# Two plain float32 pieces in block 0's first layer, all of W1 centred by means, loads on two queues, and a new written order

## The chip, the cores and the metric

One core of a Trainium2 chip. The time is device microseconds of one execution, the median of several runs. The kernel keeps all its engines under one written order: TensorE (PE) multiplies, VectorE (DVE), ScalarE (ACT) and GpSimd (POOL) do the elementwise work, SyncE (SP) issues the loads and stores.

## What is computed

A linear attention with decay over 4 batches, 8 heads and 768 tokens, in chunks, and on its output a normalised two-layer network with a residual:

```python
# attention, per chunk: y = ((C B^T) * L) x + (C state) * decay ;  state = decay * state + (B * decay)^T x
mu = np.mean(x, axis=-1, keepdims=True)
var = np.mean((x - mu) ** 2, axis=-1, keepdims=True)
xn = (x - mu) / np.sqrt(var + 1e-06) * g_ln
ch = np.maximum(xn @ w_ch1, 0.0) @ w_ch2          # 256 -> 1024 -> 256
return (x + ch).astype(np.float32)
```

## The kernel before

Tokens are cut into six blocks `t` of 128 tokens x 4 batches, so every matrix of a block has 512 columns. Per block the attention runs as scores `G`, weighting `R`, entering state `Vi`, values `V`, chunk sums `Z` and states `S`; `y` copies its result out of PSUM, `T` turns it by token, and the network follows: the first layer in eight pieces `h t m` of 128 rows, the second in four outputs `o t b` (for block 0 gathered in steps `oc 0 c j` that use one quarter of W2 at a time).

Precision is kept by splitting: a float32 value is an upper part in a short format (`wh` for weights, `yh` for values, `hh` for hidden values) and the rest (`wl`, `yl`, `hl`). A piece `h` multiplies upper by upper, lower by upper and upper by lower, over two halves k of 256 rows: six products of 512 columns (`hidden`, line 507).

The weights arrive as 64-bit words whose float32 content has to be decoded. For each of four tiles of W1 (`1 c k`: column half c, row half k) and four of W2 the steps are: `k0` (ACT) the magnitude, `k1` a clamp, `k2` a shift and `k3` the sign, all three on DVE, `kr` (ACT) the rest of the low word, and `f`, the sum of both, on DVE or POOL. The normalisation is folded into W1: W1 is centred over its rows. Half c=1 is centred on PE by products with `gd`, a diagonal less a mean (`wc`, line 237); half c=0 by a product that gives the mean (`wm`, line 242) and an addition on DVE (`wf`, line 247). Then `wh` and `wl` split it.

Other steps that are named here: `du` decays from the middle of a chunk, `cx`, `cm`, `C` scale C by them, `B` and `be` scale B, `W` writes decays into the weighting mask, `c2` scales C for the entering state, `sb` sets the state on the diagonal, `K` keeps the decayed state, `st` and `ag` are the row statistics, `oe` scales and adds the residual, `od` stores, `ru`, `riv`, `rd`, `ro`, `rcl` prepare the decays of later blocks, `fill` is an idle product on PE, `pc i` a tiny load on SP that waits for another load to land.

What sets the order: a string ISSUE, line 584, is read piece by piece; each engine gets its pieces in that order and works them off in that order. A letter behind a colon names the engine (`v` DVE, `p` POOL, `a` ACT, `s` SP); without one each step has a default. Tiles take a buffer from a pool that holds a set number; PE's first layer, the means and the outputs share three PSUM buffers (`ps_ffn`), freed when `hl`, `wf` or `oe` has read them.

Of the kernel before, what the change touches and what calls it, by code (L numbers as in the profile page):

```python
# [659 lines left out]
```

## Time and profile before

| | us |
|---|---|
| runs | 194.98, 195.91, 197.56 (median 195.91) |
| profiled execution, its own time | 194.59 |
| its span, first to last instruction | 192.6 |
| busy: PE, DVE, ACT, POOL | 185.3, 134.3, 67.4, 27.8 |
| share of the span: PE, DVE, ACT, POOL | 96%, 70%, 35%, 14% |
| granted TensorE clock | 1.00 throughout |

The span leaves out some 2 us of each execution ahead of the first and behind the last instruction. Busy time of PE counts pipelined products whose ends are modelled, so it says that PE had work and not that it was at its peak. A busy share over the whole span is an average over stretches that differ.

### The profile page before, as it was taken

Reading aid. Unit: us, or ns where it says so; the run is one execution under the profiler, and the core shown is the slowest. Engines: PE = TensorE matmul, PEld = TensorE weight load, DVE = VectorE, ACT = ScalarE, POOL = GpSimd, SP = SyncE. Lnnn points to the kernel's source line nnn. Section 1 sums busy time; section 2 is a strip of 40 time slices with the busy share of each in tenths; the row PEclk is TensorE's granted clock in tenths of the full one; section 3 lists DMA queues with packets and bytes.
Section 4 is the critical chain, followed back from the end, with each engine's and each line's share of the span. In section 5 each row is a group of like instructions: output and inputs, shape, how many; then the busy total and the mean of one; then the engine's idle time right before and its main releaser. Section 6 shows DMA issues by size and latency. Waiting matters only on the chain.

```text
span 192.6 us, 6374 instructions
## 1 busy us (share of the span) xinstructions
PE 185.3 (96%) x2834; PEld 159.2 (83%) x2834; DVE 134.3 (70%) x282; ACT 67.4 (35%) x132; POOL 27.8 (14%) x32
## 2 busy tenths in 40 slices
PE   8989799999999899999999999999999999999993
...
DVE  1699999999889687868899955636433772359321
...
DMA packets 11665, 18.42 MB, mean 96 GB/s; under 512 B 2390, under 2 KB 5878, under 8 KB 11638
## 3 DMA queue, kind: packets, MB, share of 16 engines
...
q8 instruction: 22, 0.36, 0.8%
...
## 4 chain that ended last, share of the span: by engine, by line
PE 82%; DMA 7%; DVE 4%; SPq 3%; issue 2%; POOL 1%; POOLq 0%
PE ph L513 32%; PE po L531 29%; PE yps L421 4%; DMA xt<-in_x_dram 4%; DMA b<-in_bn_dram 3%; PE yt L482 3%; PE G L394 3%; PE yps L413 3%; PE Z L433 2%; PE pp L541 2%; PE wc L240 2%; SPq L164 1%; SPq L149 1%; PE wm L245 1%; POOL top L225 1%
## 5 line engine op out<-in xcount | busy, mean ns | idle before, releaser
L531 PE MATMUL po<-w,hh 128*128 128x256 f32 x320 | 57.2, 281 | 0.0
L513 PE MATMUL ph<-yh,w 128*128 128x512 f32 x192 | 53.6, 401 | 0.5 <-DVE hl L524 0.5
L531 PEld LDWEIGHTS po<-w,hh 128*128 128x128 f32 x320 | 49.1, 188 | 0.7
L531 PE MATMUL po<-w,hl 128*128 128x256 f32 x160 | 44.7, 279 | 0.0
L513 PEld LDWEIGHTS ph<-yh,w 128*128 128x128 f32 x192 | 34.6, 188 | 8.3 <-DVE hl L524 0.9
L524 DVE SCALAR_TENSOR_TENSOR hl<-ph,hh 128x512 fp32r<-128x512 f32 x48 | 32.5, 680 | 9.9 <-ACT hh L518 9.6
L518 ACT ACTIVATE hh<-ph 128x512 fp32r<-128x512 f32 x33 | 19.4, 597 | 49.4 <-PE ph L513 42.5
L531 PEld LDWEIGHTS po<-w,hl 128*128 128x128 f32 x160 | 30.1, 188 | 0.0
L513 PE MATMUL ph<-yl,w 128*128 128x512 f32 x96 | 29.8, 391 | 0.0
L546 DVE SCALAR_TENSOR_TENSOR o<-po,rstd,ytok 128x256 f32<-128x256 f32 x20 | 9.5, 480 | 21.7 <-PE po L531 21.6
L513 PEld LDWEIGHTS ph<-yl,w 128*128 128x128 f32 x96 | 18.0, 188 | 4.0
L474 POOL TENSOR_TENSOR yl<-y,yh 128x512 fp32r<-128x512 f32 x6 | 8.1, 1351 | 59.7 <-DVE yh L471 37.9
L400 DVE TENSOR_TENSOR R<-G,WW 128x512 f32<-128x512 f32 x24 | 15.7, 678 | 1.1 <-PE G L394 1.1
L520 DVE TENSOR_SCALAR hh<-ph 128x512 fp32r<-128x512 f32 x15 | 10.3, 684 | 3.9 <-PE ph L513 3.8
L541 PE MATMUL pp<-w,hh 128*128 128x256 f32 x64 | 11.5, 281 | 0.0
L541 PEld LDWEIGHTS pp<-w,hh 128*128 128x128 f32 x64 | 9.9, 188 | 0.8 <-DVE cs L345 0.6
L457 ACT ACTIVATE sbd<-S,cst 128x128 f32<-128x128 f32 x10 | 3.5, 393 | 19.0 <-DVE S L449 19.0
L494 DVE BATCH_NORM_STATS2 st<-ytok 128x6 f32<-128x256 f32 x24 | 9.6, 413 | 0.0
L541 PE MATMUL pp<-w,hl 128*128 128x256 f32 x32 | 8.9, 279 | 0.5 <-issue 0.5
L558 PE MATMUL idle<-const-float32-0.0 128*128 128x256 f32 (+2 forms) x18 | 8.6, 601 | 0.8 <-PEq L648 0.8
L421 PE MATMUL yps<-R,xt 64*32 64x64 f32 x768 | 8.9, 225 | 0.0
L421 PEld LDWEIGHTS yps<-R,xt 64*32 64x32 f32 x768 | 7.9, 105 | 0.7 <-issue 0.4
...
## 6 DMA issues: line engine op xcount, KB each, us to landing
...
```

Of the source, the lines that this page charges most:

```text
L400: nc.vector.tensor_tensor(out=R.rearrange("p b i k -> p b (i k)"), in0=tiles.pop(("G", t, q)).rearrange("p b i k -> p b (i k)"), in1=WW.re ...
L421: nc.tensor.matmul(tiles["y", t, g, f][32 * k:32 * k + 32, b], x[r, b * NH + h], tiles["R", t, h // 2][r, b, h % 2], start=(t + f + b == 0 ...
L474: e.tensor_tensor(out=tiles["yl", t][:, g], in0=tiles["y32", t][:, g], in1=tiles["yh", t][:, g].bitcast(F32), op=ALU.subtract)
L494: nc.vector.bn_stats(out=st, in_=tiles["ytok", t][:, b])
L513: nc.tensor.matmul(ph, W1[m // 4, k][:, s, mc], v[:, k], start=(i == 0), stop=(i == len(cmb) - 1))
L518: e.activation(h, tiles["ph", t, m], AF.Relu)
L520: e.tensor_scalar(out=h, in0=tiles["ph", t, m], scalar1=0.0, scalar2=None, op0=ALU.max)
L524: nc.vector.scalar_tensor_tensor(out=l, in0=tiles.pop(("ph", t, m)), scalar=0.0, in1=tiles["hh", t, m].bitcast(F32), op0=ALU.max, op1=ALU. ...
L531: nc.tensor.matmul(po, tiles[v, t, m][:, cols], W2[m // 2,][:, s, (m % 2) * DM:(m % 2 + 1) * DM], start=(n == 0), stop=(n == len(cmb) - 1))
L541: nc.tensor.matmul(tiles["po", t, b], tiles[v, t, m][:, cols], W2[m // 2,][:, s, (m % 2) * DM:(m % 2 + 1) * DM], start=(c + n + b % 2 == 0 ...
L546: nc.vector.scalar_tensor_tensor(out=o, in0=tiles.pop(("po", t, b)), scalar=tiles["rstd", t][:, b], in1=tiles["ytok", t][:, b], op0=ALU.mu ...
L558: nc.tensor.matmul(ps[:, :n], zero.to_broadcast([P, P]), zero.to_broadcast([P, n]), start=True, stop=True)
```

## The change

Six edits. (1) Two of the eight pieces of block 0's first layer, m = 5 and 7, become `hf` (`hidden_plain`): two float32 products of the unsplit centred W1 and unsplit values. (2) Half c=1 of W1 is centred like half c=0: `wm 1`, `wf 1 0`, `wf 1 1` take the place of `wc 1 1`, `wc 1 0` and `gd`; `wh` and `wl` read it from SBUF. (3) The loads of `sel`, `sums`, `id` and `x 0` are issued by ACT. (4) The load of ACT's table moves from the start to just ahead of the logarithm. (5) Output tiles have four buffers for six, `y32` two for one; `lr` can run on DVE. (6) The whole order is written anew: which engine does what, the fills, and the `pc` loads. Cut to its core, with the orders up to the scores of block 2:

```diff
...
-    nc.scalar.preload_act_table_set("natural_log_exp_and_others")
...
-    op = pool("op", 6)
+    op = pool("op", 4)
...
-    gd = hp.tile([P, KC, P], F32, tag="hh", name="gd")
...
-    seen = cp.tile([1, 64], F32, name="seen")
+    seen = cp.tile([1, 176], F32, name="seen")
...
-    def clamped(w, *at):
+    def clamped(w, *at, e=nc.vector):
-        nc.vector.tensor_scalar(out=f, in0=f, scalar1=MIN_TOP, scalar2=MAX_TOP, op0=ALU.max, op1=ALU.min)
+        e.tensor_scalar(out=f, in0=f, scalar1=MIN_TOP, scalar2=MAX_TOP, op0=ALU.max, op1=ALU.min)
...
-    def centring(e=nc.vector):
-        if e is nc.scalar:
-            e.activation(gneg, gt, AF.Copy, scale=-1.0 / DM)
-            for k in range(KC):
-                e.activation(gd[:, k], ident, AF.Identity, bias=gneg[:, k:k + 1], scale=gt[:, k:k + 1])
-        else:
-            e.tensor_scalar(out=gneg, in0=gt, scalar1=-1.0 / DM, scalar2=None, op0=ALU.mult)
-            for k in range(KC):
-                e.tensor_scalar(out=gd[:, k], in0=ident, scalar1=gt[:, k:k + 1], scalar2=gneg[:, k:k + 1], op0=ALU.mult, op1=ALU.add)
-
-    def centred(c, k):
-        w = centre[c, k] = ps_ffn.tile([P, 512], F32, tag="ffn", name=f"wc{c}{k}")
-        for n, j in enumerate((k, 1 - k)):
-            nc.tensor.matmul(w, gd[:, k] if j == k else gneg[:, j:j + 1].to_broadcast([P, P]), f32[1, c, j], start=(n == 0), stop=(n == 1))
+    def centring(e=nc.scalar):
+        e.activation(gneg, gt, AF.Copy, scale=-1.0 / DM)
...
-        (e.copy if e is nc.scalar else e.tensor_copy)(t[:, 0], centre.get(at, f32[(w, *at)]) if w == 1 else f32[(w, *at)])
+        (e.copy if e is nc.scalar else e.tensor_copy)(t[:, 0], f32[(w, *at)])
-        e.tensor_tensor(out=t[:, 1], in0=centre.get(at, f32[(w, *at)]) if w == 1 else f32.pop((w, *at)), in1=t[:, 0].bitcast(F32), op=ALU.subtract)
+        e.tensor_tensor(out=t[:, 1], in0=f32[(w, *at)], in1=t[:, 0].bitcast(F32), op=ALU.subtract)
...
+        nc.scalar.preload_act_table_set("natural_log_exp_and_others")
...
-    def logs_repeated(t):
+    def logs_repeated(t, e=nc.scalar):
-        nc.scalar.activation(lr.rearrange("p (r n) -> p r n", n=DS), la[:, t].unsqueeze(2).to_broadcast([P, NR, DS]), AF.Copy)
+        (e.copy if e is nc.scalar else e.tensor_copy)(lr.rearrange("p (r n) -> p r n", n=DS), la[:, t].unsqueeze(2).to_broadcast([P, NR, DS]))
...
-            tiles["y32", t] = p1.tile([P, KC, TB], F32, tag="y32", name=f"y32{t}")
+            tiles["y32", t] = p2.tile([P, KC, TB], F32, tag="y32", name=f"y32{t}")
...
+
+    def hidden_plain(t, m):
+        ph = tiles["ph", t, m] = ps_ffn.tile([P, TB], F32, tag="ffn", name=f"ph{t}{m}")
+        for k in range(KC):
+            nc.tensor.matmul(ph, f32[1, m // 4, k][:, m % 4 * P:(m % 4 + 1) * P], tiles["y32", t][:, k], start=(k == 0), stop=(k == KC - 1))
...
-        k0=magnitude, k1=clamped, km=bounded, k2=shifted, k3=signed, kr=rest, f=whole, wc=centred, wm=mean_of, wf=less_mean, wh=upper, wl=lower,
+        k0=magnitude, k1=clamped, km=bounded, k2=shifted, k3=signed, kr=rest, f=whole, wm=mean_of, wf=less_mean, wh=upper, wl=lower,
-        h=hidden, hh=hidden_h, hl=hidden_l, o=outputs, oc=outputs_of, oe=finished, od=stored)
+        h=hidden, hf=hidden_plain, hh=hidden_h, hl=hidden_l, o=outputs, oc=outputs_of, oe=finished, od=stored)
...
...
-az, fill 0 512, ld la, inv, ld sums, ld mask, ld as, fill 1 512, ld b 0, l1, ini, ld id, l2, ld c 0, lr 0, ld bt 0, ones, fill 2 256, ld sel, rcl,
-ld g, ru, fill 3 64, ld w1 1 0, dc 0, ld w1 1 1, ld x 0, fill 4 256, du 0 1, e 1, du 0 0, B:v 0, fill 5 256, lr 1, so, cx 0 0, x 1, fill 6 256,
-cx 0 1, e 0, x 0, W:v 0, gm:a, G 0, pc 4 w1 1 0, k0 1 1 0, be:v 0, dc 1, ld w1 0 1, sm, k1 1 1 0, ld w1 0 0, mb, R 0 3, fill 7 512, du 1 0, ld bt 1,
-C 0, R 0 0, ld x 1, kr 1 1 0, sp, R 0 2, em 0, em 1, c2:p 0, Z 0 0, k0 1 1 1, riv, R 0 1, Z 0 1, S 0 0, k1 1 1 1, fill 8 256, sb:a 0 1, k2 1 1 0,
-k2 1 1 1, kr 1 1 1, Vi 0, k3 1 1 1, du 1 1, V 0 0, k3 1 1 0, k0 1 0 1, V 0 1, f:v 1 1 1, y 0 0 0, f:v 1 1 0, wc 1 1, y 0 1 0, kr 1 0 0, k1 1 0 1,
-ld c 2, ro 0, ld c 1, ld b 1, pc 2 w1 0 0, ld w2 0, k2 1 0 1, k0 1 0 0, k3 1 0 1, wc 1 0, be:v 1, k1 1 0 0, ld bt 2, k2 1 0 0, ld w2 2, rd, k3 1 0 0,
-ro 1, ld w2 1, f:v 1 0 0, ld x 2, K 0 1, ld b 2, C:v 1, ld ud 2, wh 1 1 1, kr 1 0 1, y 0 0 1, f 1 0 1, y 0 1 1, wh 1 1 0, T 0 1, yh:a 0 0, Z 1,
-yh:a 0 1, T 0 0, tc 0 1, yl 0 0, wm 0, W 1, wl:v 1 1 0, yl 0 1, S 0 1, wl:v 1 1 1, h 0 5, tc 0 0, K:p 1 0, wf 0 1, cm 1 1, B:v 1, h 0 4, cm 1 0,
-S 1 0, wf 0 0, k0 2 0, sb:v 1 1, G 1, hh 0 4, wh:v 1 0 1, wh 1 0 0, wl:v 1 0 1, hh 0 5, h 0 7, hl 0 4, wl 1 0 0, kr 2 0, hl 0 5, k0 2 2, R 1 0,
-h 0 3, sb 1 0, hh 0 7, R 1 2, c2:p 1, R 1 1, h 0 2, hh 0 3, K:p 1 1, hl 0 7, kr 2 1, B 2, st 0 1, S 1 1, h 0 1, R 1 3, C:v 2, k1 2 0, Vi 1, hh 0 1,
-st 0 2, cm:v 2 0, W 2, hl 0 1, V 1 0, c2 2, V 1 1, hl 0 3, h 0 0, y 1 0 1, ld x 4, k2 2 0, hh 0 2, ld w2 3, k3 2 0, y 1 0 0, ld c 3, y 1 1 1, cm 2 1,
-h 0 6, f:v 2 0, ld bt 3, yh:a 1 0, k1 2 2, K 2 0, y 1 1 0, yl:v 1 0, hh 0 0, G 2, yh:a 1 1, hl 0 2, hh 0 6, st 0 0, T 1 0, yl 1 1, R 2 3, wh 2 0,
...
+ld:a sel, fill 0 512, ld la, ld:a sums, ld mask, ld:a id, ld c 0, ld w1 1 0, fill 1 128, ld b 0, l1, fill 2 512, ini, ld bt 0, l2, ld:a x 0, lr:v 0,
+inv, ones:v, e 1, dc 0, x 1, W:v 0, so, du 0 0, fill 3 512, du 0 1, cx 0 1, sm, lr 1, mb, k0 1 1 0, cx 0 0, dc 1, ld w1 1 1, k1 1 1 0, e 0, B:v 0,
+x 0, du 1 0, C:v 0, G 0, kr 1 1 0, k2 1 1 0, be:v 0, sp, k3 1 1 0, em 0, Z 0 0, ld g, ld w1 0 0, ld as, ld c 1, ld w1 0 1, ld bt 1, ld b 1, c2:p 0,
+R 0 1, fill 4 256, S 0 0, R 0 3, sb:a 0 1, Z 0 1, f 1 1 0, R 0 0, k0 1 1 1, Vi 0, R 0 2, kr 1 1 1, V 0 0, az, k1 1 1 1, gm, du 1 1, k2 1 1 1, em 1,
+rcl, k3 1 1 1, k0 1 0 0, V 0 1, f:v 1 1 1, wm 1, y 0 1 1, pc 3 c 1, ld x 1, pc 19 c 0, pc 18 b 0, C:v 1, ld x 2, y 0 1 0, y 0 0 0, y 0 0 1, k1 1 0 0,
+cm 1 0, c2:p 1, wf 1 0, T 0 0, k0 1 0 1, T 0 1, wf 1 1, K:p 0 1, yh:a 0 0, hf 0 5, k2 1 0 0, kr 1 0 0, k1 1 0 1, ru, tc 0 1, k3 1 0 0, ro 0,
+wh 1 1 1, hf 0 7, ld w2 1, S 0 1, kr 1 0 1, k2 1 0 1, ld b 2, sb:a 1 0, be:v 1, ld w2 0, tc 0 0, k3 1 0 1, Z 1, cm 1 1, riv, f:v 1 0 1, yh:a 0 1,
+wl:v 1 1 1, hh 0 7, rd, W 1, ro 1, pc 15 b 2, wh:p 1 1 0, B 1, f 1 0 0, K:p 1 0, wm 0, yl 0 0, S 1 0, wl 1 1 0, hl 0 7, G 1, wf 0 0, ld c 2, yl 0 1,
+wf 0 1, ld bt 2, kr 2 1, h 0 4, ld ud 2, R 1 1, hh 0 5, wh:p 1 0 0, R 1 2, ld w2 2, K:p 1 1, R 1 3, h 0 6, hh 0 4, sb 1 1, S 1 1, k0 2 1, R 1 0,
+k0 2 0, Vi 1, k1 2 1, W 2, hl 0 4, hl 0 5, V 1 1, k1 2 0, V 1 0, K 2 0, k2 2 0, ld x 3, y 1 0 0, k3 2 0, y 1 1 1, ld c 3, y 1 1 0, y:v 1 0 1, hh 0 6,
+C:v 2, ld bt 3, hl 0 6, cm:v 2 0, yh 1 0, B:v 2, pc 11 w2 1, ld w2 3, ld ud 3, pc 13 w2 3, ld ud 4, ld b 3, wh:p 1 0 1, wl 1 0 0, wl 1 0 1, h 0 1,
+sb 2 0, be 2, h 0 0, hh 0 1, c2:p 2, cm 2 1, h 0 3, hh 0 0, yh:a 1 1, yl 1 0, hl 0 0, G 2, hh 0 3, k2 2 1, kr 2 0, yl 1 1, T 1 0, R 2 3, h 1 4,
+tc 1 0, hl 0 3, k3 2 1, h 1 2, f:v 2 0, hh 1 4, f 2 1, R 2 0, hl 1 4, Z 2, R 2 2, wh 2 1, T 1 1, hh 1 2, hl 0 1, h 0 2, st 0 0, wh:v 2 0, S 2 0,
+wl 2 0, h 1 3, sb:a 2 1, hh:v 0 2, kr 2 3, hl 0 2, tc 1 1, oc 0 0 1, K 2 1, kr 2 2, st 0 3, S 2 1, k0 2 2, ag 0 0, C:v 3, h 1 6, R 2 1, wl:v 2 1,
...
```

## Rows read from the trace of the kernel before

**Rows 1.** The page's 40 equal slices of the span, busy tenths.

```profile
PE   8989799999999899999999999999999999999993
DVE  1699999999889687868899955636433772359321
```

**Rows 2.** Busy us of each engine (instructions) in two stretches, clock, DMA share, GB/s.

```profile
20.00:25.00 5.00, 3.64 (x77) 2.15 (x76) 4.93 (x10) 3.52 (x9) 2.43 (x2) 1.00 0.87 295
30.00:35.00 5.00, 5.00 (x34) 4.05 (x22) 5.00 (x10) 3.69 (x7) 4.49 (x5) 1.00 0.22 75
```

**Rows 3.** The chain that ended last, in order: start us, us, what.

```profile
17.50 3.20 PE wc L240 x7
20.70 1.36 issue
24.57 1.72 PE wm L245 x4
...
43.05 2.78 PE ph L513 x12
...
189.25 0.48 DVE o L546
```

**Rows 4.** PE's instructions in order: start us, us, what, count, idle before.

```profile
25.72 1.50 PE L513 MATMUL ph<-yh,w 128*128 128x512 f32 x4
30.12 1.20 PE L513 MATMUL ph<-yh,w 128*128 128x512 f32 x4
41.26 1.21 PE L394 MATMUL G<-cm,bs 32*64 32x128 f32 x64
57.30 0.28 PE L541 MATMUL pp<-w,hl 128*128 128x256 f32 x1 [0.47 <-issue]
66.43 1.20 PE L513 MATMUL ph<-yh,w 128*128 128x512 f32 x4 [0.53 <-DVE hl L524]
```

**Rows 5.** The opening, in order of time: table load, fills, a load's issue.

```profile
0.73 1.28 ACT L82 ACT_TABLE_LOAD   x1 [0.73 <-PEq L648]
0.77 4.92 PE L558 MATMUL idle<-const-float32-0.0 128*128 128x512 f32 x8 [0.77 <-PEq L648]
1.18 0.42 SPq L164 DMA_DIRECT2D cf<-in_sums_dram  x1
1.76 0.34 PEld L558 LDWEIGHTS idle<-const-float32-0.0 128*128 128x128 f32 x1 [0.52 <-issue]
```

**Rows 6.** DVE and POOL side by side, in order of time.

```profile
20.86 1.40 POOL L225 TENSOR_TENSOR top<-top,low 128x512 int32<-128x512 int32 x1 [6.42 <-ACT low L220]
21.12 1.69 DVE L214 SCALAR_TENSOR_TENSOR top<-raw,top 128x512 int32<-128x512 int32 x1
...
31.56 1.88 DVE L400 TENSOR_TENSOR R<-G,WW 128x512 f32<-128x512 f32 x3
31.77 0.63 POOL L459 TENSOR_TENSOR sbd<-S,cst 128x256 f32<-128x256 f32 x1
...
44.80 0.64 POOL L459 TENSOR_TENSOR sbd<-S,cst 128x256 f32<-128x256 f32 x1
45.20 0.79 DVE L258 TENSOR_TENSOR w<-top,w 128x512 fp32r<-128x512 f32 x1
...
113.79 1.06 POOL L441 TENSOR_TENSOR K<-S,emt 128x256 f32<-128x256 f32 x1 [16.54 <-DVE S L449]
```

**Rows 7.** Groups by line and shape: count, busy us, mean ns of one, idle before.

```profile
L214 DVE SCALAR_TENSOR_TENSOR top<-raw,top 128x512 int32<-128x512 int32 x8 | 6.4, 805 | 0.1
L225 POOL TENSOR_TENSOR top<-top,low 128x512 int32<-128x512 int32 x3 | 4.0, 1326 | 7.4 <-ACT low L220 6.4 <-DVE top L214 1.0
L258 DVE TENSOR_TENSOR w<-top,w 128x512 fp32r<-128x512 f32 x5 | 3.6, 711 | 0.2
L368 POOL TENSOR_TENSOR c<-cs,em 128x512 f32<-128x512 f32 x4 | 4.2, 1049 | 22.4 <-DVE cs L345 22.4
L209 DVE TENSOR_SCALAR top<-top 128x512 int32<-128x512 int32 x8 | 3.3, 418 | 0.1
L441 POOL TENSOR_TENSOR K<-S,emt 128x256 f32<-128x256 f32 x5 | 3.5, 702 | 23.8 <-DVE S L449 23.8
```

More of the change, by code (lines that the diff above doesn't have):

```diff
@@ L617 @@
-oe 4 2, hh:v 5 1, hl 5 1, h 5 3, oe 4 1, od 4 1, h 5 0, hh 5 3, hl 5 3, h 5 4, hh 5 0, hl 5 0, h 5 6, hh:v 5 4, hl 5 4, h 5 7, ag 5 1, hh:v 5 6,
-hl 5 6, h 5 5, st 5 2, st 5 0, st 5 3, hh:v 5 7, hh 5 5, ag 5 2, hl 5 7, hl 5 5, o 5 2, ag 5 0, ag 5 3, rs 5, rc 5, o 5 1, o 5 3, oe 5 1, od 5 1,
-od 4 2, od 3 0, o 5 0, oe 5 3, oe 5 2, od 5 3, od 3 2, od 0 3, od 5 2, oe 5 0, od 5 0
+ld:a sel, fill 0 512, ld la, ld:a sums, ld mask, ld:a id, ld c 0, ld w1 1 0, fill 1 128, ld b 0, l1, fill 2 512, ini, ld bt 0, l2, ld:a x 0, lr:v 0,
```

41 lines of the change are left out of this document (21 added, 20 removed).

## Prediction, made before the changed kernel ran

> **What bounds the kernel now.** I read the page's 40 slices first, then the busy time by stretch, then the chain that ended last, and last the single instructions of VectorE and GpSimd. TensorE (PE) is busy in every slice but the first ones and the last [rows 1]. The stretches say what kind of busy it is: from 20 to 25 us PE is busy 3.64 us of 5 while VectorE (DVE) is busy 4.93; from 30 to 35 PE is at 5.00 of 5 and so is DVE [rows 2]. So the front, until the first layer of block 0 can start at 25.72 us, is paced by DVE; from there PE is full, and DVE runs close behind it until about 60 us and is half idle later [rows 1, 2, 4]. After 25.72 PE loses 1.0 us in two short waits, 0.47 ahead of 57.30 and 0.53 ahead of 66.43 [rows 4]. The last product ends at 189.2 us, one scaled addition of DVE and the stores follow, and the span ends at 192.6 [rows 3]. A gain must therefore come from an earlier, or a less broken, first part; PE idle time anywhere ahead of 189 us is lost for good, since PE works in written order.
>
> **What each matrix edit costs PE.** A first-layer piece with both values split is six products: twelve in 2.78 us, so 1.39 a piece. The mean of W1's half c is two float32 products that run as four instructions, 1.72 us [rows 3]. A plain piece `hf` is the same shape, so 1.72: two of them add 2 x 0.33 = +0.66 us. Replacing `wc 1 1` and `wc 1 0` (eight instructions, seven took 3.20, so 3.7 with the last [rows 3]) by one `wm 1` removes about 1.9 us. The fills shrink from 2880 to 1920 columns; they stood in the front, where PE waits anyway. Sum on PE about -1.2 us, all of it in the front, where PE doesn't set the pace: worth nothing by itself. The gain of `hf` is another: it needs no `wh`, `wl`, `yh`, `yl`, only float32 values and the centred half, so it can start earlier.
>
> **The front, along DVE.** ACT now issues three loads ahead of the table load. An issue takes 0.42 on SP, nearest row for ACT [rows 5]; from 0.73 three take until 2.1, the table 1.28 [rows 5] until 3.4, the logarithm after it (0.36) ends near 3.8. `lr:v 0`, `inv` and `ones:v` (0.6, 0.1, about 0.8 by its 1024 elements) fill DVE while it would wait for `x 1`, which hides them. `W:v 0` starts near 5.5. From there to the end of `wf 1 1` DVE has W 1.13, cx 2 x 0.65, B, C 0, be, k3, k3, f, C 1 at 0.60 each, four R at 0.60, six small ones at 0.34 (k1, k2 and `rcl`, 0.42 each [rows 7]), wf 2 x 0.66: 12.4 us with 0.7 of waits for ACT's `du` and `k0`, so about 18.7 us (start to start of operations in a row is 0.07 under the duration: three R in 1.88 [rows 6]). [...] The two plain pieces can run from 18.7 to 22, against a first piece at 25.72 before. This is the promise of the change, 6 to 7 us early; the question is whether the next piece follows.
>
> **What holds it back: GpSimd.** The new order moves work from DVE to GpSimd (POOL): counted over the two orders, `wl` 5 for 1, `wh` and `yh` 5 for none, `yl` 9 for 6, `sb` 4 for 2, one more each of be, K and W, one `c2` less: 43 operations for 27. POOL takes 1.33 us for a sum of 128x512, DVE 0.71 for the like [rows 7]; 16 more at some 1.1 are 18 us of POOL for about 9 of DVE and ACT. And the two don't run side by side. `k3` on DVE at 21.12 took 1.69 us, the other seven (6.4 - 1.69)/7 = 0.67: POOL's `f` lasted until 22.26 and `k3` ended 0.55 after it. `wl:v` at 45.20 took 0.79 while POOL's `sb` lasted until 45.44. In the other direction POOL's `K` of 113.79 took 1.06, behind a `yl:v` of DVE, where the mean of five is 0.70. The three R under POOL's work at 31.56 lost nothing: they read PSUM [rows 6, 7]. So a DVE operation with two SBUF inputs, or a fast single-input one, and a POOL operation exclude each other for their full length; DVE operations that read PSUM (R, S, hl, wf) are free. The order of before puts POOL's work under those. [...]
>
> [...] DVE: k2, k1, ru, k2 (4 x 0.34), k3, be 1, k3, f:v (4 x 0.60), 3.8 us. POOL, all needed soon: `wh:p 1 1 0` about 1.0 (not in the trace; between half of a two-input 1.30 and the whole; I take nearer the whole, since `c2` with one broadcast input takes 1.05 [rows 7]), B 1, f, yl and wl, each with two inputs, at 1.3 and K at 0.6 [rows 6, 7] (`sb`, as wide as K, 0.63), 6.8 us. Waiting engines take turns: POOL's `f` dispatched at 20.86 got in ahead of `k3` at 21.12 [rows 6]. So `f:v 1 0 1` ends at 18.7 + 10.6 = 29.4 (rounded up 0.1), not at 22.8. Behind it the second half of `wm 0` (0.86), G 1 (1.14): 31.4. Z 1 and `wm 0` stand in PE's order ahead of everything else, so PE idles between 22 and 31 for some 5 us. The third piece, `h 0 4`, also needs one of three PSUM buffers, freed by `hl 0 7`, which DVE reaches after yl (1.3 POOL), wl, rd, S, hl (1.9): 32.6. Before, the third piece started at 30.12 [rows 4]: +2.5 us.
>
> Next, `wl 1 0 1` gates piece (0,1): from 33.2 (`wf 0 0`) POOL does wh:p, K, sb, wh:p, wl, wl (5.8) and one k1 (0.34) gets between: 39.4. Then DVE, behind `hl 0 4` and `hl 0 5` (39.3), shares with sb 2 0 and be 2: 0.6 + 0.34 + 1.05 + K, k2, k3, y, C 2, hl, cm, yh, B 2 (4.6): B 2 ends near 45.9, and G 2 starts there. Before, G 2 started at 41.26 [rows 4] with eight pieces done; now with seven, so the same place would be 41.26 - 1.39 = 39.9. That is 6.0 us late. Behind it PE has more waiting for it than DVE, as now; the two waits of 1.0 us may vanish: +5.0.
>
> **The rest of the edits.** Four output buffers for six: the new order never holds more than four tiles, and a whole product `o` stands between a store and the next use of its buffer; nothing, and without that cover about the length of one addition, 0.48 [rows 3], a few times. The second `y32` buffer and the six tiny SP loads `pc` for three: SP waits there instead of elsewhere; what is queued behind are loads of block 2 and 3, needed after 40 us. x 0 on ACT's queue is needed at 11 us, by then under way for 7. Tail unchanged, 3.4 us. All at zero.
>
> **Sum.** Span 192.6 + 5.0 = 197.6. The profiled execution of before took 194.59, so 199.6 for one like it; the median shown is 195.91, 1.3 above, so I predict 200.9 us.
>
> **Rivals.** (1) The other side: POOL's operations fall under DVE's PSUM reads and cost DVE nothing. It decides if `f:v 1 0 1` ends before 25 us. Then `wm 0` ends at 23.7, G 1 at 24.9, the third piece starts at 25.5 instead of 30.12; `wl 1 0 1` at 32.5 and G 2 at about 36.2 against 39.9: 3.7 us early, and with the two vanished waits -4.7: 191.2. For it: the order of before shows that such packing works [rows 6]; against it: behind `wf 1 1` the new order has ten DVE operations in a row of which one reads PSUM. [...] (3) On top of the forecast PE falls to the slow pace: it was slow for its first 4.9 us [rows 5] and didn't fall after a wait of 1.36 us at 20.7 [rows 3]; the idle times I expect are longer. [...] Each fall costs at most the 2.5 us that 4.9 us at half pace lose: one to two falls, 203 to 206.
>
> **Chances.** Forecast (198.5 to 203) 0.42; rival 1 0.22; rival 2 0.22; rival 3 0.14. 2%, about what a measurement of this kernel can tell from no change, is 3.9 us: below 192.0 or above 199.8. Of rival 1, 0.17 lies below and 0.05 inside; rival 2 lies inside, and so does 0.10 of the forecast, its low end: faster 0.17, same 0.37, slower 0.46. Range: from rival 1's own figure, 191.2, to a little above rival 3's, 207.0; that leaves about 0.11 below and 0.03 above.
>
> **What would show it.** Right: `hf` near 19 to 20 us; then PE idle of several us before Z 1 and G 1; durations over 1 us among DVE's k1, k2, k3, be of 20 to 30 us and among POOL's; `h 0 4` after 31; G 2 after 44. Wrong, if POOL's busy time rises by 15 us and DVE's durations stay at 0.4 and 0.7, if G 2 starts before 40, or if a wait for a load or a store stands in the chain.

## The result: 1.2% slower, half of the forecast loss

| | before | after |
|---|---|---|
| median of 20 runs each, us | 195.91 (194.46 to 198.12) | 198.40 (196.70 to 201.06) |
| ratio, 95% interval | | 1.012 [1.0086, 1.0155] |
| profiled execution: time, span, us | 194.59, 192.6 | 200.21, 198.4 |
| busy: PE, DVE, ACT, POOL, us | 185.3, 134.3, 67.4, 27.8 | 188.9, 135.0, 64.5, 45.8 |

The change costs 2.5 us by the medians; 5.0 were forecast. The ratios leave out executions more than 1.5% above the quickest of their kernel, the medians are over all. The profiled execution of after is one of the longer of its twenty, so a second profile of the same kernel (`a0`, time 198.06, span 196.3) is used beside it; its four runs had a median of 198.98 and a ratio to before of 1.0225 [1.0155, 1.0295].

After, the page's 40 slices (they answer to [rows 1]):

```profile
PE   8997959997999999999999999999999999999993
DVE  3795599999999974877599684557441784238420
POOL 0043377767421290250000150200000500000000
PEclk9995795899999999999999999999999999999999
```

PE shows holes in the fourth and the sixth slice (15 to 20 and 25 to 30 us), the granted clock falls twice between 15 and 40 us (0.50 from 16 to 22, 0.53 from 29 to 36), and POOL is busy in the slices in which DVE is full. The stretches (busy us of PE, PEld, DVE, ACT, POOL, granted clock, DMA share, GB/s; [rows 2] has two of them before):

```profile
15.00:20.00 5.00, 3.63 (x116) 2.46 (x116) 2.74 (x6) 2.59 (x9) 1.73 (x2) 0.57 0.52 170
20.00:25.00 5.00, 5.00 (x16) 2.80 (x15) 2.96 (x4) 3.38 (x7) 2.07 (x2) 0.74 0.17 62
30.00:35.00 5.00, 4.66 (x26) 1.57 (x34) 4.96 (x7) 2.40 (x4) 3.32 (x2) 0.50 0.27 103
```

PE's instructions in order, after ([rows 4] before):

```profile
14.65 0.34 PE L408 MATMUL yps<-R,xt 64*32 64x64 f32 x14
16.37 1.86 PE L408 MATMUL yps<-R,xt 64*32 64x64 f32 x114 [1.39 <-issue]
18.16 3.78 PE L231 MATMUL wm<-top,gneg 128*128 128x512 f32 x4
23.03 3.60 PE L505 MATMUL ph<-y,top 128*128 128x512 f32 x8
...
28.89 1.01 PE L420 MATMUL Z<-xt,be 64*32 64x64 f32 x64 [2.26 <-DVE be L360]
...
34.25 2.20 PE L381 MATMUL G<-cm,bs 32*64 32x128 f32 x64
36.39 1.18 PE L500 MATMUL ph<-yh,w 128*128 128x512 f32 x4
...
47.50 1.23 PE L381 MATMUL G<-cm,bs 32*64 32x128 f32 x64 [0.24 <-DVE bs L351]
```

Line 408 is `V 0`, line 231 `wm`, line 505 the plain pieces `hf`, line 500 a split piece. G 2 starts at 47.50 here and at 45.33 in the second profile; forecast 45.9, before 41.26 [rows 4]. But the way there is another one: PE waits 1.39 us within `V 0 0` for nothing that the profile shows, the four instructions of `wm 1` take 3.78 us where a `wm` before took 1.72 [rows 3], and `hf` starts at 23, not 18.7. Behind G 2 PE has no wait worth naming; the last product ends at 195.3.

DVE and POOL side by side, after ([rows 6] before). On DVE line 198 is `k1`, 207 `k2`, 212 `k3`, 223 `f`, 235 `wf`, 360 `be`; on POOL 351 is `B`, 223 `f`, 461 `yl`, 244 `wl`:

```profile
22.04 1.41 DVE L235 SCALAR_TENSOR_TENSOR top<-top,gt,wm 128x512 f32<-128x512 f32 x2 [4.15 <-issue]
...
23.42 1.50 POOL L351 TENSOR_TENSOR bs<-b,ud 128x512 f32<-128x512 f32 x1
23.70 1.51 DVE L198 TENSOR_SCALAR top<-top 128x512 f32<-128x512 f32 x1
...
26.27 1.26 POOL L223 TENSOR_TENSOR top<-top,low 128x512 int32<-128x512 int32 x1 [1.34 <-DVE top L212]
26.38 1.44 DVE L207 TENSOR_SCALAR top<-top 128x512 int32<-128x512 int32 x1
27.73 1.10 DVE L360 TENSOR_TENSOR be<-bt,pend 128x512 f32<-128x512 f32 x1
...
28.25 1.72 POOL L461 TENSOR_TENSOR yl<-y,yh 128x512 fp32r<-128x512 f32 x1
28.75 1.76 DVE L212 SCALAR_TENSOR_TENSOR top<-raw,top 128x512 int32<-128x512 int32 x1
29.93 1.71 POOL L244 TENSOR_TENSOR w<-top,w 128x512 fp32r<-128x512 f32 x1
30.65 1.54 DVE L223 CUSTOM_DVE_ANT_0 top<-top,low 128x1024 uint16<-128x1024 uint16 x1
```

The four DVE operations here that meet a whole sum of POOL (k1, k2, k3, f) take 0.9 to 1.1 us longer than alone, and `be`, which meets the half as wide `K`, 0.4; the two engines take turns, as forecast. The groups that answer to [rows 7] say the same as means for k2 (418 ns before) and less for a sum `f` on POOL (1326) and its `K` (702), beside the new cast `wh:p`:

```profile
L207 DVE TENSOR_SCALAR top<-top 128x512 int32<-128x512 int32 x8 | 4.9, 607 | 0.1
L223 POOL TENSOR_TENSOR top<-top,low 128x512 int32<-128x512 int32 x3 | 4.2, 1407 | 2.1 <-DVE top L212 2.1
L428 POOL TENSOR_TENSOR K<-S,emt 128x256 f32<-128x256 f32 x6 | 4.3, 718 | 4.5 <-DVE S L436 4.5
L240 POOL CAST w<-top 128x512 fp32r<-128x512 f32 x3 | 1.8, 611 | 6.0 <-DVE top L235 6.0
```

### The profile page after: what moved, and what is told of

Its sections match the earlier page's. It is cut to its first block, busy times and chain, and to the rows that moved or that the text cites. A ratio compares the mean times of both kernels' runs of the same rounds, so it can differ in the third digit from the quotient of the medians.

```text
span 198.4 us, 6336 instructions
## 1 busy us (share of the span) xinstructions
PE 188.9 (95%) x2818; PEld 158.9 (80%) x2818; DVE 135.0 (68%) x271; ACT 64.5 (32%) x128; POOL 45.8 (23%) x48
## 4 chain that ended last, share of the span: by engine, by line
PE 80%; DVE 10%; issue 5%; POOL 2%; ACT 1%; POOLq 0%
PE ph L500 29%; PE po L523 28%; PE pp L533 6%; PE G L381 4%; PE yps L408 3%; PE yt L469 3%; PE yps L400 2%; PE idle L550 2%; PE Z L420 1%; DVE top L198 1%; DVE R L387 1%; DVE top L212 1%; POOL c L355 1%; DVE top L207 1%; PE wm L231 1%
## 5 line engine op out<-in xcount | busy, mean ns | idle before, releaser
L500 PE MATMUL ph<-yh,w 128*128 128x512 f32 x184 | 51.1, 399 | 0.8 <-DVE hl L516 0.8
L510 ACT ACTIVATE hh<-ph 128x512 fp32r<-128x512 f32 x34 | 20.1, 597 | 73.4 <-PE ph L500 72.2
L516 DVE SCALAR_TENSOR_TENSOR hl<-ph,hh 128x512 fp32r<-128x512 f32 x48 | 32.4, 682 | 13.8 <-ACT hh L510 13.5
L500 PEld LDWEIGHTS ph<-yh,w 128*128 128x128 f32 x184 | 32.8, 188 | 7.8 <-DVE hl L516 1.2
L500 PE MATMUL ph<-yl,w 128*128 128x512 f32 x92 | 28.5, 391 | 0.0
L461 POOL TENSOR_TENSOR yl<-y,yh 128x512 fp32r<-128x512 f32 x9 | 12.9, 1442 | 42.4 <-PE ph L500 27.4
L500 PEld LDWEIGHTS ph<-yl,w 128*128 128x128 f32 x92 | 17.3, 188 | 3.8
L512 DVE TENSOR_SCALAR hh<-ph 128x512 fp32r<-128x512 f32 x14 | 9.6, 686 | 0.8 <-PE ph L500 0.5
L452 ACT COPY y<-yps 128x256 f32<-128x256 f32 x17 | 5.6, 378 | 12.5 <-PE yps L408 12.3
L244 POOL TENSOR_TENSOR w<-top,w 128x512 fp32r<-128x512 f32 x5 | 7.4, 1484 | 9.9 <-ACT hh L510 7.9
L381 PEld LDWEIGHTS G<-cm,bs 32*64 32x64 f32 x384 | 6.8, 144 | 3.5 <-issue 2.5
```

Source lines behind the costliest of these rows:

```text
L381: nc.tensor.matmul(G[q][f * HALF:(f + 1) * HALF, b], bs[r, tok], cm[r, :, tok], start=True, stop=True)
L461: e.tensor_tensor(out=tiles["yl", t][:, g], in0=tiles["y32", t][:, g], in1=tiles["yh", t][:, g].bitcast(F32), op=ALU.subtract)
L500: nc.tensor.matmul(ph, W1[m // 4, k][:, s, mc], v[:, k], start=(i == 0), stop=(i == len(cmb) - 1))
L510: e.activation(h, tiles["ph", t, m], AF.Relu)
L512: e.tensor_scalar(out=h, in0=tiles["ph", t, m], scalar1=0.0, scalar2=None, op0=ALU.max)
L516: nc.vector.scalar_tensor_tensor(out=l, in0=tiles.pop(("ph", t, m)), scalar=0.0, in1=tiles["hh", t, m].bitcast(F32), op0=ALU.max, op1=ALU. ...
```

## The experiments

Two theories. **Theory 1**: DVE and POOL exclude each other, and their sum from `wf 1 1` to `B 2` sets G 2. **Theory 2**: PE's wait and half pace around `V 0 0` and `wm` (granted clock 0.50 in the profile of after) set it. All kernels below were built from one of the two and timed beside the kernel before. `a0` already speaks against the half pace alone: its clock stayed at 1.00 up to 27.9 us, and its span is 3.7 us longer than before.

**The whole loss in one table.** Worked out from each profile: when the 16 KB packet of instructions that precedes `V 0 0` crosses (the transfer view, instruction queue, in slices of 0.1 us), PE's wait in `V 0 0`, the end of `wf 1 1` (start plus duration of its row), the start of G 2, and what is left from there to the span's end.

| kernel | packet | wait | wf 1 1 ends | G 2 | wf 1 1 to G 2 | G 2 to end |
|---|---|---|---|---|---|---|
| after | 13.9 | 1.39 | 23.45 | 47.50 | 24.05 | 150.9 |
| a0 (after again) | 13.9 | 1.45 | 21.17 | 45.33 | 24.16 | 151.0 |
| a1 (after again) | 14.5 | 2.00 | 23.96 | 47.94 | 23.98 | 151.2 |
| e4 kept warm | 14.8 | 2.03 | 24.23 | 48.20 | 23.97 | 153.1 |
| e2 paced, `as` late | 12.2 | none | 22.70 | 46.70 | 24.00 | 151.2 |
| e8 paced | 12.1 | none | 20.14 | 44.32 | 24.18 | 151.3 |
| e1 splits off POOL | 13.8 | 1.66 | 20.98 | 44.01 | 23.03 | 151.2 |
| e3 POOL light | 11.9 | none | 19.25 | 41.73 | 22.48 | 151.4 |
| e7 light and paced | 11.2 | none | 19.18 | 41.35 | 22.17 | 152.0 |

Three terms make the time: when `wf 1 1` ends, a stretch to G 2 that depends on the order, and 151 to 152 us from G 2 on (before: 192.6 - 41.26 = 151.3). The last term holds only while no new wait of PE comes behind G 2: it is 153.1 in e4 and 155.7 in e5 and e6, further below.

### Is it the exclusion? e1, e3

e1 takes the weight splitting ahead of G 2 off POOL (the steps that move, gathered from several places of the order):

```diff
-wh:p 1 1 0, wl 1 1 0, wh:p 1 0 0, wh:p 1 0 1, wl 1 0 0, wl 1 0 1
+wh 1 1 0, wl:v 1 1 0, wh 1 0 0, wh 1 0 1, wl:v 1 0 0, wl:v 1 0 1
```

> The changed kernel with the splitting of W1 taken off POOL: three wh go to ACT, three wl to DVE. Theory 1: 3 x 0.61 + 3 x 1.3 = 5.7 us leave the path that POOL and DVE share and 3 x 0.6 = 1.8 us come to it, so G 2 starts up to 3.9 us earlier, and the kernel is 2 to 4 us faster than the changed one, at or below the time of before. Theory 2: DVE has 1.8 us more to do ahead of G 2, POOL's part was hidden: 0 to 1.8 us slower than the changed kernel.

Measured 196.99 against 198.98 of the changed kernel beside it; ratio to before 1.0087 [1.0037, 1.0137] against 1.0225 [1.0155, 1.0295]. `wf 1 1` to G 2 took 23.03 for 24.16, with the wait still there. G 2 came at 44.01, 1.3 us earlier than in `a0`; up to 3.9 were expected, and the time of before was not reached.

e3 goes on from e1, takes off the sums too, and puts `be 2`, which stays on POOL, from ahead of G 2 to behind `yl 1 1`:

```diff
-f 1 0 0, K:p 1 0, yl 0 0, yl 0 1, be 2
+f:v 1 0 0, K 1 0, yl:v 0 0, yl:v 0 1, be 2
```

> The changed kernel with nearly all of GpSimd's work ahead of G 2 taken off it: as in the run that split on ACT and VectorE, and on top f 1 0 0, yl 0 0, yl 0 1 and K 1 0 on VectorE, and be 2 behind yl 1 1. Theory 1: the two engines exclude each other, so each sum that moves costs VectorE 0.6 and gives back the 1.3 that GpSimd held; f 1.27, K 0.80 and two yl 3.39 go and 0.6 + 0.34 + 2 x 0.6 come, so G 1 starts some 2.5 to 3 us ahead of the 30.5 of that run, be 2 gives 0.8 more, and G 2 comes at 41 to 42 instead of 44.0: about 2 to 3 us faster than that run, level with the kernel before or 1 us faster. Rival (GpSimd's work ran beside VectorE and VectorE is the longer one): VectorE gets 2.1 us more, and the run is 1 to 2 us slower than that run.

Measured 196.03, ratio 0.9995 [0.9958, 1.0033]: level with before, G 2 at 41.73, as expected; below e1 it is 1.0 us by the medians, less than the 2 to 3 expected. DVE has more to do than in the changed kernel and is done sooner. Its operations in this profile, `be` and `k3`, which took 1.10 and 1.76 above:

```profile
22.35 0.68 DVE L360 TENSOR_TENSOR be<-bt,pend 128x512 f32<-128x512 f32 x1
22.95 0.68 DVE L212 SCALAR_TENSOR_TENSOR top<-raw,top 128x512 int32<-128x512 int32 x1
```

One reserve: in this profile the wait of PE was absent, so of its 3.6 us at G 2 against `a0` 1.7 belong to the shorter stretch and 1.9 to the earlier start.

### What one operation of POOL costs: p1, p2

Into the kernel before, where POOL is idle (behind `f:v 1 1 0`), go three more sums (p1), or six casts (p2):

```diff
+        nc.gpsimd.tensor_tensor(out=extra, in0=f32[1, 1, 1], in1=f32[1, 1, 1], op=ALU.add)
```

```diff
+        nc.gpsimd.tensor_copy(extra, f32[1, 1, 1])
```

> The kernel before with three more sums of 128x512 on GpSimd (result unused), behind f 1 1 0 in the order, when GpSimd has nothing else to do (it is idle from 14.4 to 20.9 us). They can start at about 17.4. Theory 1 (exclusion): VectorE has only SBUF operations then; three times 1.3 us of its time go, the front ends 3.5 to 4 us later, G 2 too, and the run is 3 to 4 us slower (1.015 to 1.02). Rival (engines run side by side): GpSimd's own f 1 0 1 starts 0.3 us later, and the time stays within 0.5 us. At half the price: 1.5 to 2 us.

> The kernel before with six casts of 128x512 on GpSimd in the place of the three sums of the other run (result unused): 6 x 0.61 = 3.7 us of GpSimd, as much as the three sums. If a cast excludes VectorE like a sum does: 3 to 4 us slower, as there. If the exclusion is one of two inputs, and a cast costs VectorE nothing: f 1 0 1 of GpSimd starts 0.2 to 0.9 us later, and the run is 0 to 0.9 us slower.

p1: 199.63 against 196.17, ratio 1.0236 [1.0156, 1.0317]. p2: 201.44 against 196.75, ratio 1.0240 [1.0171, 1.0309]. Work on an idle engine, whose result nobody reads, makes the kernel before 2.4% slower, twice what the whole change does. The casts, too, exclude. POOL and DVE in p1:

```profile
17.28 3.78 POOL L230 TENSOR_TENSOR extra<-top 128x512 f32<-128x512 f32 x3 [2.96 <-DVE top L225]
...
19.02 1.15 DVE L209 TENSOR_SCALAR top<-top 128x512 int32<-128x512 int32 x1
20.20 1.41 DVE L214 SCALAR_TENSOR_TENSOR top<-raw,top 128x512 int32<-128x512 int32 x1
...
27.89 2.75 PE L250 MATMUL wm<-top,gneg 128*128 128x512 f32 x4 [3.63 <-DVE top L225]
```

and in p2:

```profile
17.27 5.29 POOL L230 CAST extra<-top 128x512 fp32r<-128x512 f32 x6 [2.95 <-DVE top L225]
...
18.59 0.72 DVE L209 TENSOR_SCALAR top<-top 128x512 int32<-128x512 int32 x1
19.35 0.97 DVE L214 SCALAR_TENSOR_TENSOR top<-raw,top 128x512 int32<-128x512 int32 x1
```

The sums keep their own pace (3.78 / 3 = 1.26) while k2 takes 1.15 for 0.42 and k3 1.41 for 0.67: 0.73 to 0.74 of DVE's time each, not 1.26. A cast takes 0.88 here and 0.61 where nothing of DVE excludes it. Not all of the loss is theirs, though: in p1 DVE is 2.1 us late behind the three sums (`be` starts at 21.53 for 19.39, 0.45 of it a wait for ACT) and 4.3 us late at the end of `f:v 1 0 0` (27.83 for 23.54), because `f` and `yl` of POOL now meet other operations, and PE falls to the slow pace after a wait of 3.63 (granted clock 0.50 from 29 to 32 us).

### PE's wait: e2, e4, e8, a1

e2 holds loads on SP (a `pc` makes SP wait for another load to land) so that the wait, if it comes from full transfer queues, goes:

```diff
-ld g, ld w1 0 0, ld as, ld c 1
+ld g, pc 5 w1 1 1, ld w1 0 0, pc 6 w1 0 0, ld as, ld c 1
```

> The changed kernel with two tiny loads more on SP, so that w1 0 0 waits for w1 1 1 to land and the loads behind it for w1 0 0: less is under way at 12 to 16 us. If PE's wait of 1.39 us at 15 us comes from the loads that are under way beside it, it falls below 0.5 us, the clock stays at 1.00 until 25 us, wf 1 1 ends near 19 us (23.4 in the profile of the changed kernel) and the kernel is 1 to 3 us faster than the changed one. If the loads have no part in it, the wait stays at 1.2 to 1.5 us and the time within 0.5 us.

Measured 200.03, ratio 1.0257 [1.0217, 1.0298]. The wait in `V 0 0` went, as expected, but `wf 1 1` ended at 22.70 and not near 19, and no time was gained. Another wait came: `as` stood behind the held loads on SP, and `rcl`, which reads it, stands in DVE's order ahead of `k3` and `f`; PE, which needs `f` for `wm 1`, stood idle 2.07 us and fell to the slow pace from 20.8 to 24 us (mean granted clock of the span 0.991).

```profile
18.11 0.23 DVE L316 TENSOR_SCALAR AZs<-as 128x124 f32<-128x124 f32 x1 [2.16 <-DMA as<-in_as_dram]
```

e8 lets `as` and `c 1` go first and holds only what is needed late:

```diff
-ld g, ld w1 0 0, ld as, ld c 1, ld w1 0 1, ld bt 1, ld b 1
+ld g, ld as, ld c 1, pc 5 w1 1 1, ld w1 0 0, ld w1 0 1, ld bt 1, ld b 1
```

> The changed kernel with the loads of W1's half 0 and of bt 1, b 1 held on SP until w1 1 1 has landed, as and c 1 ahead of them; nothing else. Theory of the late code: PE's instructions for V 0 0 land before 12.5 us, the wait at the 15th product of V 0 0 goes, wf 1 1 ends at 19 to 19.5 instead of 21.1 to 24.2, G 2 follows 24.1 us later (43.1 to 43.6), the end 151.1 us after that: span 194.5, time 196 to 196.5, 2 to 2.5 us below the changed kernel of the same call, and no run above 199 us. Rival (the loads that are held come late instead, at k0 1 0 0 or G 1): no gain, within 0.5 us.

> The changed kernel once more, unchanged, beside the two others on the same chip. If the size of the change hangs on when the code lands, its times keep the spread of 196.7 to 201 us; where wf 1 1 ends in the profile tells which it was, and G 2 comes 24.1 us after it.

e8: 197.24 (195.65 to 197.63, 12 runs), ratio 1.0069 [1.0031, 1.0107]. a1, the changed kernel on the same chip: 200.51 (197.47 to 201.80, 6 runs), ratio 1.0201 [1.0107, 1.0295]. One line of SP's order is worth 1.3% by these ratios, and the spread goes with it. Against the first measurement of the changed kernel (1.012) it is 0.5%, and against `a0` (1.0225) 1.6%. The time is 1 us above the expected 196 to 196.5: `wf 1 1` ended at 20.14 and not at 19 to 19.5, G 2 came at 44.32 and not at 43.1 to 43.6. PE in e8:

```profile
15.07 1.65 PE L408 MATMUL yps<-R,xt 64*32 64x64 f32 x128
16.65 1.98 PE L231 MATMUL wm<-top,gneg 128*128 128x512 f32 x4
...
21.15 3.16 PE L505 MATMUL ph<-y,top 128*128 128x512 f32 x7 [0.93 <-issue]
...
44.32 1.20 PE L381 MATMUL G<-cm,bs 32*64 32x128 f32 x64 [0.24 <-DVE bs L351]
```

All 128 products of `V 0 0` and `V 0 1` run without a break, `wm 1` runs at full pace (1.98 us for its four, 3.78 in the profile of after), and the stretch to G 2 (24.18) is that of the changed kernel, although the clock hardly falls here (mean of the span 0.996, 0.966 in the profile of after). A wait of the same kind has come in the plain pieces instead (0.93 us), behind the next packet of the instruction queue, at 18.7; behind these pieces PE waits for DVE all the same (1.41 us ahead of `Z 1`).

e4 keeps PE busy in the gap behind the plain pieces, with idle products into the buffer that `wm 0` is about to overwrite:

```diff
+wk 5 256, Z 1, wk 3 256, wm 0
+            nc.tensor.matmul(w[:, :n], zero.to_broadcast([P, P]), zero.to_broadcast([P, n]), start=True, stop=True)
```

> The changed kernel with eight idle products of 256 columns in the gap of TensorE behind the plain pieces (five ahead of Z 1, three ahead of wm 0), written into the buffer that wm 0 is about to overwrite. They keep PE busy where it stood idle for 2.3 and 1.0 us. Theory 1 (VectorE and GpSimd pace the front): the products of wm 0 and G 1 run at full pace, G 1 ends 1 to 2 us earlier, but G 2 waits for B 2 on VectorE as before; time within 0.5 us of the changed kernel. Theory 2 (what PE's slow pace costs sets the end): every execution with a fall near 29 us gains what its products of 29 to 36 us lost, about 2 us, and the runs above 199 us go.

Measured 203.31, ratio 1.0406 [1.0339, 1.0474]. PE ran at full pace from 25 us on (granted clock 0.50 from 17 to 23 us, 1.00 from 24 to 25), and the stretch from `wf 1 1` to G 2 took 23.97 us for 24.05 and 24.16 with a fall: PE's pace there costs nothing. That the time would stay within 0.5 us of the changed kernel was wrong. Two waits are in its profile: 2.03 us in `V 0 0` behind a packet at 14.8, like the 2.00 of `a1`, and a new one, within another `V` much later (the added products and their weight loads are 32 instructions):

```profile
114.44 0.30 PE L414 MATMUL yps<-R,xt 64*32 64x64 f32 x3 [1.54 <-issue]
```

### The matrix edit, the two queues, and the way to a better order: b2, b1, e5, e6, e7, e9, f1

b2 has the plain pieces and the mean of half 1 in the order of before:

```diff
-wc 1 1, wc 1 0, h 0 5, h 0 4
+wm 1, wf 1 0, wf 1 1, hf 0 5, hf 0 4
```

> The kernel before with edits (1) and (2) alone, in its own order: wm 1, wf 1 0 and wf 1 1 stand where the two wc stood, and two of the pieces (m = 5 and 4) are plain ones that run right behind the second T. Theory 1 (the front goes by the sum of VectorE's own operations and of those of GpSimd that exclude it): the two wf add 2 x 0.7 = 1.4 us to VectorE ahead of G 1, nothing else changes there, so G 1 starts at about 30.4 instead of 28.98, G 2 about 1.4 later than 41.26, and the run is 1 to 1.5 us slower. Theory of the cheaper matrix work (PE loses 1.2 us in the front and gains the gap ahead of 25.7): G 2 1 to 2 us earlier and the run 1 to 2 us faster.

Measured 200.25, ratio 1.0249 [1.0186, 1.0312]; G 2 at 46.40, 5 us late and not 1.4. The values that the plain pieces read come late in ACT's order there, so T waits 2.99 us, PE falls to the slow pace (the plain pieces take 5.29 us, 3.60 in the profile of after), and the pieces stand in front of `Z 1` and `wm 0`:

```profile
22.83 1.26 PE L482 MATMUL yt<-cst,y 128*128 128x128 f32 x8 [2.99 <-ACT y L465]
23.93 5.29 PE L518 MATMUL ph<-y,top 128*128 128x512 f32 x8
```

So the edit needs an order of its own; b2 doesn't price the edit alone.

b1 gives the kernel before the loads on ACT and the late table load.

```diff
-    nc.scalar.preload_act_table_set("natural_log_exp_and_others")
-ld sums, ld id, ld sel, ld x 0
+ld:a sel, ld:a sums, ld:a id, ld:a x 0
```

> The kernel before with one part of the change alone: sel, sums, id and x 0 loaded by ACT, three of them ahead of the table load, which moves to just ahead of the logarithm. By the prediction's step the logarithm ends 0.3 to 0.4 us later, which old fills on PE hide: within 0.5 us of before. A rival is that the loads of SP land up to 1 us earlier: 0.5 to 1 us faster.

Measured 196.22 against 196.29, ratio 1.0026 [0.9983, 1.0070]: what these two edits are worth can't be told from nothing, as the prediction has it.

e5 moves four decoding steps of W2 behind G 2 and two copies to ACT, from e3; e6 adds the pacing of e8.

```diff
-k1 2 1, k1 2 0, k2 2 0, k3 2 0, cm:v 2 0, yh 1 0
+cm 2 0, yh:a 1 0, B:v 2, hl 0 0, k1 2 1, k1 2 0, R 2 3, k2 2 0, k3 2 0
```

> The run with little on GpSimd, and beside it four decoding steps of W2 (k1 2 1, k1 2 0, k2 2 0, k3 2 0) moved from ahead of B 2 to behind hl 0 0 and R 2 3, and cm 2 0 and yh 1 0 from VectorE to ScalarE. Theory 1 (what VectorE has to do ahead of B 2 sets G 2, and from G 2 to the end every run takes 151.1 us): 0.34 x 3 + 0.60 + 0.9 + 0.34 = 2.9 us less on VectorE, of which PE's own pieces eat some: G 2 1.5 to 2.5 us earlier than 41.73, and the run 1.5 to 2.5 us faster than that run, so 1 us or more faster than the kernel before. Rival (PE's pieces and ScalarE's copies set G 2 by then): no more than 0.5 us.

> The same, and the loads of W1's half 0 and of bt 1, b 1 held on SP until w1 1 1 has landed (as and c 1 go ahead of them). Theory of the late code (PE's wait of 1.4 to 2.0 us in V 0 0 is for its 16 KB of instructions, whose packet comes late when the transfer queues are full around 10 to 14 us): the packet lands before 12.5, there is no wait at the 15th product of V 0 0, wf 1 1 ends at 19 to 19.5 in every execution, the spread of the times shrinks to about 1.5 us, and the median is 0.5 to 1.5 us below that of the run without the pacing. Rival (the wait comes from something else): wait and spread as there.

e5: 199.18, 1.0122 [1.0047, 1.0197]; e6: 198.96, 1.0125 [1.0052, 1.0199]. The stretch from `wf 1 1` to G 2 shortened as expected (19.73 in e5, 20.50 in e6), with G 2 at 43.63 in e5, behind a late `wf 1 1`, and at 39.97 in e6. The gain was given back at once: the two k1 (2.72 and 2.71 us beside POOL's `yl`) stand ahead of `hl 0 3`, and PE waits for its buffer.

```profile
49.99 2.00 PE L500 MATMUL ph<-yh,w 128*128 128x512 f32 x4 [3.18 <-DVE hl L516]
```

That line is of e5; e6 has the same wait. The packet came at 14.3 in e5 and at 11.6 in e6, with 1.78 us of wait in `V 0 0` and none. But of the 0.5 to 1.5 us that this was expected to bring, the medians show 0.2, and the spread (2.3 us, four runs) did not shrink to 1.5. This expectation failed, and why is open: the traces are of e5's longest execution and e6's shortest.

e7 is e3 with the pacing of e8 and the two copies on ACT; W2's steps stay where they were.

```diff
-cm:v 2 0, yh 1 0
+cm 2 0, yh:a 1 0
```

> The run with little on GpSimd, with cm 2 0 and yh 1 0 on ScalarE (1.3 us less on VectorE ahead of G 2) and the same held loads; the steps of W2 stay where they were. Theory 1 with the late code: wf 1 1 ends at 19 to 19.5, G 2 21.5 us later (40.5 to 41), time 194 to 194.5, about 1 to 1.5 us below the kernel before of the same call and with less spread. Rival (PE's own pieces or ScalarE's copies set G 2): level with the kernel before.

195.57 (195.13 to 196.46, 12 runs), ratio 1.0012 [0.9977, 1.0047]: level with the kernel before, which spread from 194.04 to 198.38 beside it; 1 to 1.5 us less were expected. It ran beside e8, and the two hold the same loads: e8's median is 1.7 us above it, the price of the work on POOL (and of two copies on DVE). G 2 is only 0.4 earlier than in e3, since with `yh` on ACT `yl` starts sooner on POOL and meets `B 2` (1.25 us for 0.68).

e9 moves `K 1 0` and `S 1 0` forward in e7; f1 moves the one sum of POOL that collides in the kernel before to DVE, and a `pc` of SP ahead of three loads.

```diff
-f:v 1 0 1, wl:v 1 1 1, wl:v 1 1 0, rd, K 1 0, S 1 0
+f:v 1 0 1, K 1 0, S 1 0, wl:v 1 1 1, wl:v 1 1 0, rd
```

```diff
-ld c 2, ld c 1, ld b 1, pc 2 w1 0 0, f 1 0 1
+pc 2 w1 0 0, ld c 2, ld c 1, ld b 1, f:v 1 0 1
```

> The run with little on GpSimd and held loads, with K 1 0 and S 1 0 right behind f 1 0 1 on VectorE instead of behind wl 1 1 0 and rd: S 1 0 is what TensorE waits for inside G 1 (0.63 us). Theory 1 (VectorE's order up to B 2 sets G 2): G 1 ends up to 0.6 us earlier, but the same operations stand ahead of B 2, so G 2 stays within 0.3 us of 41.35, and the time within 0.3 us. Rival (PE's waits add up to the end whatever VectorE does): 0.6 us faster.

> The kernel before with its one sum f 1 0 1 moved from GpSimd to VectorE (behind K 0 1), and the wait for w1 0 0 on SP ahead of the loads of c 2, c 1 and b 1. Exclusion: k3 1 0 0 takes 0.67 instead of 1.69 and f 0.60 comes, so VectorE is 0.4 us earlier at C 1; if that paces the front, G 2 comes 0.3 to 0.5 us earlier than in the kernel before and the time is 0.3 to 0.8 us lower. Rival (the sum was free on GpSimd): 0.6 us later at C 1, time 0.3 to 0.6 us higher.

e9: 196.72, 1.0059 [1.0029, 1.0090]: 0.5% above e7 by the ratios, whose intervals overlap. A wait of 0.63 is gone and one of 1.32 for `hl` has come in its place; G 2 was expected within 0.3 us of 41.35 and came at 42.81, of which 0.9 us is a later `wf 1 1`. f1: 197.22, 1.0038 [0.9996, 1.0080], the difference not told from none, where 0.3 to 0.8 us less were expected. There k3 fell to 0.67 as expected, but then `f` met POOL's `yl` and took 1.77. No version can be told from the kernel before as faster.

## Why the prediction was right or wrong

**Right: the mechanism named and the sign.** POOL's busy time rose by 18.0 us, DVE's k1, k2, k3, be and f of that stretch took 1.1 to 1.8 us, and `hf` was followed by idle time of PE. Rival 1 (POOL hidden) falls with p1, e1 and e3. But exclusion is only a part of the loss: 1.7 us by e8 against e7. The rest goes with PE's wait in `V 0 0`, which the prediction did not have (e8 against `a1`). That G 2 came at 45.33 in `a0` for 45.9 is luck: a stretch forecast 3.0 us too long stood behind a start forecast 2.5 us too early. Of the edits put at nothing, ACT's loads and the table can't be told from nothing (b1); the buffers were not tested alone, but PE was busy throughout behind G 2. The engines take turns, as the prediction said, but the traces show less than exclusion for the full length: a pair of two-input operations took 1.68 us, and not the 1.90 of both lengths. No row of [rows 6] shows a single-input operation of DVE beside POOL; `k1` and `k2` do in the profile of after (1.51 and 1.44 us for 0.42).

**Wrong: the size, by four terms that partly cancel** (in us, against `a0`). The steps that failed are the sum of the exclusive stretch, and the statement that PE doesn't set the pace in the front. Two rows of `a0` that the first term rests on, the first `wh:p` and the end of `f:v 1 0 1`:

```profile
20.57 0.61 POOL L240 CAST w<-top 128x512 fp32r<-128x512 f32 x1 [1.26 <-DVE top L235]
...
28.36 1.54 DVE L223 CUSTOM_DVE_ANT_0 top<-top,low 128x1024 uint16<-128x1024 uint16 x1
```

1. *The exclusive stretch was summed too long: 27.2 forecast from `wf 1 1` to G 2, 24.16 measured, -3.0.* Up to `f:v 1 0 1` it was 10.7 forecast and 29.90 - 21.17 = 8.7 measured. The sum took each operation of POOL at its full length. `wh:p` was taken at 1.0 and took 0.61, and the first of them ran under the second `wf`, which reads PSUM, and ended with it (21.18 against 21.17): all of its 1.0 falls out. In the row of two-input operations, `yl` and `wl` of POOL start 1.68 apart (28.25, 29.93 in the profile of after), with one operation of DVE in turn with each (k3, then f): 1.68 a pair, and not 0.60 + 1.30. The rest of the stretch, to `wl 1 0 1` and G 2, is 1.1 shorter, 0.8 of it by two `wh:p` at 0.61.
2. *`wf 1 1` was put at 18.7 and ended at 21.17, +2.5 (23.45 in the profile of after).* Here the step failed that said PE doesn't set the pace in the front. DVE was some 0.5 us behind the forecast (`k1 1 0 0` ended at 17.83, and 18.7 less the two `wf` is 17.4); then it waited 1.92 us in `a0`, and 4.15 in the profile of after, for `wm 1`, which stood behind PE's wait. The prediction saw the like of it before (1.36 us of "issue" in [rows 3]) and used it only as a sign about the clock. e8 shows the price: without this wait `wf 1 1` ended at 20.14, 1.0 earlier than in `a0` and 3.8 earlier than in `a1`, and the time is 0.5 to 1.6% less. The other 1.4 us to the forecast's 18.7 is there without it too: 0.9 of it is a later `k1 1 0 0`, 0.4 a wait for `wm 1`.
3. *Behind G 2, -0.7.* Forecast 151.34 + 1.39 - 1.0 = 151.7, measured 151.0. The two waits named were not all: from 50 to 190 us PE was busy 138.2 of 140 before, and all 140 after, so 1.8 us of idle time went and not 1.0.
4. *The 1.3 us for the median, -1.3.* The profiled execution of before was among its quickest three of twenty. That it lay 1.3 below the median was carried over to after, where `a0` (198.06) lies close to the median (198.40). b1, which is the kernel before but for its opening, had G 2 at 42.71 in its profile and not 41.26: the delay is to be counted from about 42.6 (41.26 + 1.3).

Together 5.0 - 3.0 + 2.5 - 0.7 = 3.8 between `a0` and the profile of before (196.3 - 192.6 = 3.7), and less 1.3 the 2.5 of the medians. Of the chances, the measured 1.2% falls under same, which had 0.37 against 0.46 for slower. The half pace that rival 3 counts with is in the trace of before: the weight loads of the first fills start 0.85 us apart (1.76, 2.61, 3.46 us), where a product of `wm` takes 0.43 (1.72 for four). Rival 3 has a fall after the idle time behind `hf`: it came (28 to 35 us in `a0`, 29 to 36 in the profile of after, there at a granted clock of 0.53) and costs nothing, since the stretch to G 2 is as long without it (e4, e8). The fall that costs is another, 16 to 22 us in the profile of after, at a granted clock of 0.50, behind the wait of 1.39: 2.3 us (23.45 - 21.17 at nearly the same wait), where DVE waits for PE's products.

**Open.** The clock fell to 0.50 behind waits of 1.39, 1.78, 2.00 and 2.03 us in `V 0 0` and stayed at 1.00 behind 1.45 and 1.66, and behind the 1.36 before; what decides it no run here tells. Nor what makes the packet cross at 13.8 to 14.8 in six profiles without held loads and at 11.9 in a seventh (e3), where all issue the same loads in the same order up to then; only that it crosses at 11.2 to 12.2 in five profiles of five with held loads (e9's 11.9 is the fifth). What the wait is worth in the time is open too: 0.5 to 1.6% by e8, next to nothing by the medians of e5 and e6.
